# B units over 128 rows in a spectral layer and ELU kernel: Y regrouped from SBUF to SBUF

## The chip, the core and the metric

The kernel runs on one core of one Trainium2 chip. A time is the device microseconds of one execution. Before the change three runs took 894.23, 894.43 and 895.2 us; the median is 894.43 us.

## What is computed

Eight sequences of 3008 rows by 256 channels are transformed along the rows, mixed over channels by a complex matrix, shrunk, transformed back, and put through a two-layer network with an ELU between:

```python
X = np.fft.rfft(x, axis=1)
Yr = Xr @ w_r - Xi @ w_i + b_r
Yi = Xr @ w_i + Xi @ w_r + b_i
Y  = sign(Y) * max(|Y| - 0.01, 0)          # real and imaginary part each
y  = np.fft.irfft(Y, n=3008, axis=1)
h  = y @ w_in                              # 256 -> 2048
out = where(h > 0, h, exp(min(h, 0)) - 1) @ w_out   # 2048 -> 256
```

## The kernel before

3008 is 47 x 64, and each transform is done in two factors, as matrix products with small constant matrices M1 to M4. For one sequence (a "batch" here) the spectral part is a list of units, each a few matmuls and one move out of PSUM:

- A units (`unit_A`, L170 matmuls): first factor of the forward transform; stored to DRAM (DA) and loaded again as Z.
- X units (`unit_X`, L207): second factor; gives XT.
- M units (`unit_M`, q = 0..5, i = 0, 1; L247 in batch 1, L289 from batch 2 on): channel mixing and shrinking. The PSUM result goes through VectorE (L257, or L144 and L296) and then GpSimd (L269 and L270, or L301, L302 and L303), which writes one half of the tile Y(q): 128 partitions, two frequencies pp, real and imaginary part c, 256 channels.
- B units (`unit_B`, v = 0..5; L375): first factor of the inverse transform on Y(v). Partitions 0 to 63 of Y hold one parity s of the frequencies, 64 to 127 the other. The two parities are separate products over 64 rows; for each, the real and the imaginary part are added up in PSUM. That makes eight matmuls of 64 rows by 256 columns for a unit: 2 (pp) x 2 (c) x 2 (s). The result is copied to Bz (L144 or L146), every second unit stored to DRAM (DB, L400), and loaded again as Bs (`load_Bs`, L408) after unit B5.
- Y units (`unit_Y`, L538): second factor of the inverse transform; gives yT, the network's input.

The network runs in steps: one step is four matmuls of the first layer (`front`, L1006), exponential and ELU on ScalarE, VectorE and GpSimd (L1022 to L1061), and eight fp32 matmuls of the second layer (`back`, L1080), two steps later. There are 47 steps for a batch (`PER`), and every eighth one copies osb out of PSUM (L1092) and stores it (L1101).

The order is written out by hand in `plan(b)`: while the network works on batch b, the list `seq` gives to each step one unit of batch b + 1, or an A unit of batch b + 2. `f0[t]` holds what a step emits ahead of its first-layer matmuls, `f1[t]` what it emits between them and its second-layer matmuls. Every engine takes its instructions in the order in which they were emitted. All stores and most loads are issued by SyncE (SP); the loads of x (xt, L117) by GpSimd. SP's DMAs use eight completion semaphores in turn, and one of them may have to wait until the DMA eight places before it has landed.

PSUM for X, B, A and Y units is one buffer of two banks (`psF`, tag fps), so that a unit waits until the one before it has been copied out. Batch 0 is worked off ahead of the steps and has functions of its own (`split_B`, L426; `turn_B`, L470); they stay with 64 rows.

Of the kernel before, what the change touches and what calls it, by code (L numbers as in the profile page):

```python
# [20 lines left out]
N2 = 64  # L21
K1 = 24
# [7 lines left out]
def kernel(  # L30
# [25 lines left out]
    constp = ctx.enter_context(tc.tile_pool(name="constp", bufs=1))  # L56
    M1 = constp.tile([P, P], F32R, name="M1")
    M2 = constp.tile([2 * NR, NS, 2, 2 * K1], BF16, name="M2")
    M3 = constp.tile([P, K1 // 2, 2, P], BF16, name="M3")
# [6 lines left out]
    bias_p = constp.tile([P, 2 * D], BF16, name="bias_p")  # L66
# [10 lines left out]
    space = constp.tile([P, 384], BF16, name="space")  # L77
# [24 lines left out]
    Z_of = {}  # L102
    XT_of = {}
    Y_of = {}
    Bz_of = {}
    DB_of = {}
    Bs_of = {}
# [119 lines left out]

    def sum_of(dt, ch):

        return XS[:, 3 * dt + ch] if 3 * dt + ch < 5 else busy[:]  # L230

    def three_weights(c, dt):

# [6 lines left out]
    def m_group(b, q, i, ps, biased=False):  # L240
        XT = XT_of[b]
        o = (2 * q + i) * P
        todo = [(c, dt) for c in range(2) for dt in range(2)]
        if b == 0:
            todo.sort(key=lambda z: z[1])
        for c, dt in todo:
            nc.tensor.matmul(  # L247
                ps, lhsT=XT[:, dt, c, o : o + P], rhs=(wcat_r, wcat_s)[c][:, dt, :],
                start=(not biased and (c, dt) == (0, 0)), stop=((c, dt) == (1, 1)),
            )  # L250
        if i == 0:
            Y_of[b, q] = wk3.tile([P, 2, 2 * D], BF16, name="Y", tag="Y")
        if biased:
            yb = ps
        else:
            yb = wk3.tile([P, 2 * D], F32, name="yb", tag="yb")[:]
            nc.vector.tensor_tensor(yb, ps, bias_bc[:], ALU.add)  # L257
        if (b, q, i) == (0, 2, 0):
            clip = late3.tile([P, 2 * D], F32, name="gT", tag="gT")
        else:  # L260
            clip = wk2.tile([P, 2 * D], F32, name="clip", tag="clip")
        return yb, clip

    def unit_M(b, q, i):
        if b == 1:
            if i == 0:
                mps_of[q] = unit_ps("mps", False)
            yb, clip = m_group(b, q, i, mps_of[q][:, i, :])
            nc.gpsimd.tensor_scalar(clip[:], yb, LAM, -LAM, ALU.min, ALU.max)  # L269
            nc.gpsimd.tensor_tensor(Y_of[b, q][:, i, :], yb, clip[:], ALU.subtract)  # L270
            return
        XT, o = XT_of[b], (2 * q + i) * P
        if i == 0:
            Y_of[b, q] = wk3.tile([P, 2, 2 * D], BF16, name="Y", tag="Y")
# [12 lines left out]
        for out_, lhs, w in todo:  # L287
            for dt in range(2):
                nc.tensor.matmul(  # L289
                    out_, lhsT=lhs[:, dt] if lhs is not None else sum_of(dt, ch)[:, oc : oc + P],  # L290
                    rhs=w[:, dt, :], start=(dt == 0), stop=(dt == 1),
                )
# [10 lines left out]
        nc.gpsimd.tensor_tensor(Y_of[b, q][:, i, :], yb[:], clip[:], ALU.subtract)  # L303
# [30 lines left out]
    def last_M(q, i):  # L334
# [26 lines left out]
        for Y_, yb, ch in todo:  # L361
            nc.vector.scalar_tensor_tensor(Y_, yb, LAM, ch, ALU.add, ALU.min)

    def unit_B(b, v, alone=False, on_dve=False, all_dve=False):
        if (b, v // 2) not in Bz_of:
            t = "A" if alone and v == 0 else "Bz"
            Bz_of[b, v // 2] = wk2.tile([P, 8, D], BF16, name=t, tag=t)
            if b not in DB_of:
                DB_of[b] = dram.tile([K1, P, D], BF16, name="DB", tag="DB")
        Bz, Y = Bz_of[b, v // 2], Y_of.pop((b, v))  # L370
        ps = unit_ps("bps", alone)
        for pp in range(2):
            for c in range(2):
                for s in range(2):
                    nc.tensor.matmul(  # L375
                        ps[:, s, pp * D : pp * D + D],
                        lhsT=M3[s * N2 : s * N2 + N2, 2 * v + pp, c, :],
                        rhs=Y[s * N2 : s * N2 + N2, pp, c * D : c * D + D],
                        start=(c == 0), stop=(c == 1),
                    )  # L380
# [33 lines left out]
    def split_B(v, ps, on_dve=(False, True), by_half=False):  # L414
# [8 lines left out]
        def half(pp):  # L423
            for c in range(2):
                for s in range(2):
                    nc.tensor.matmul(  # L426
                        ps[s][:, pp * D : pp * D + D],
                        lhsT=M3[s * N2 : s * N2 + N2, 2 * v + pp, c, :],
                        rhs=Y[s * N2 : s * N2 + N2, pp, c * D : c * D + D],
                        start=(c == 0), stop=(c == 1),  # L430
                    )
# [22 lines left out]
    def turn_B(v, ts=(0, 1), ps=None, on_dve=False):  # L454
# [11 lines left out]
        for pp in range(2):  # L466
            for dt in ts:
                for c in range(2):
                    for s in range(2):
# [7 lines left out]
                            rhs=M3[s * N2 : s * N2 + N2, 2 * v + pp, c, :].rearrange(  # L477
                                "p (g m) -> p g m", g=4
                            )[:, :, 0:8],
                            start=(c == 0), stop=(c == 1),  # L480
# [69 lines left out]
    def idle_pe(n):  # L550

        for _ in range(n):
            nc.tensor.matmul(ips[:], lhsT=busy[:, 0:P], rhs=busy[:], start=True, stop=True)

    nc.vector.memset(bias_p[:], 0.0)
    bpd = dram.tile([3, 2 * D], BF16, name="bpd", tag="bpd")
    idle_pe(9)
# [272 lines left out]
    XS = sump.tile([P, 5, 512], BF16, name="XS")  # L830
# [60 lines left out]
    for o, src, sc, bi in ((1, w3, TURN, 0.0), (0, a3, -TURN, hpi[:])):  # L891
        if o == 0:
            nc.scalar.activation(a3[:], w3[:], AF.Abs)
        nc.scalar.activation(
            M3[:, :, 0, o * N2 : o * N2 + N2], src[:], AF.Sin, bias=bi, scale=sc
        )
    sgb = sg3[:].unsqueeze(2).to_broadcast([P, K1 // 2, N2])
    first_M(3, 0, True)
    nc.vector.scalar_tensor_tensor(
        M3[:, :, 1, 0:N2], M3[:, :, 0, N2:P], 2.0, sgb, ALU.mult, ALU.mult  # L900
    )
    nc.vector.scalar_tensor_tensor(
        M3[:, :, 1, N2:P], M3[:, :, 0, 0:N2], -2.0, sgb, ALU.mult, ALU.mult
    )
    first_M(3, 1, True)
    let_go()
# [203 lines left out]
    def plan(b):  # L1110
# [5 lines left out]
        mid = [("X", u) for u in range(8)] + [  # L1116
# [4 lines left out]
        ]  # L1121
        if n1 < B:
            if b:
                lead, xs = 0, (3, 6, 9) if b < 3 else (3, 8, 13)

                def M(q):
                    return [("M", q, 0), ("M", q, 1)]
# [1 line left out]
                shift = b - 1 if b < 3 else b - 3  # L1129
                seq = [("y", 2), ("y", 3)] + [None] * shift + [("X", u) for u in range(8)]  # L1130
                if b < 3:
                    seq += [("y", 4)] + M(0) + M(1) + [("y", 5), ("B", 0)]
                else:
                    seq += M(0) + [("y", 4)] + M(1) + [("y", 5), ("B", 0)]
                seq += M(2) + [("y", 6), ("B", 1)] + M(3) + [("y", 7), ("B", 2)]
                on_act = [("X", 4), ("X", 7), ("B", 3)] + [("y", u) for u in range(5, 8)]
                if b < 3:
                    on_act += [("A", 0)]
                    seq += M(4) + [("B", 3)] + M(5) + [("A", 0), ("B", 4), ("B", 5)]
                    seq += [("A", u) for u in range(1, 6)]  # L1140
                else:
                    on_act += [("y", 4), ("B", 4)]
                    seq += M(4) + [("B", 3), ("A", 0)] + M(5) + [("B", 4), ("A", 1), ("B", 5)]
                    seq += [("A", u) for u in range(2, 6)] + [None] * (3 if n2 == B else 2)
                seq += [("n", 0), ("n", 1)]
            else:
                lead, seq = FILL, (
                    [u for u in mid if u[0] != "A"]
                    + [("A", 0), ("A", 1), ("A", 2), ("n", 0), ("n", 1)]
                    + [("A", u) for u in range(3, 6)]  # L1150
                )
# [3 lines left out]
        for t, u in enumerate(seq, lead):  # L1155
# [16 lines left out]
                    f0[t].append(put("A", n2, u[1]))  # L1172
            else:
                f0[t].append(put(u[0], n1, *u[1:]))
            if u == ("B", 5):
                f1[t + (b > 0 and n2 < B)] += [
                    (load_Bs, (n1, w, 0, 4 * K1 - 16 * (b == w == 0))) for w in range(4)
# [4 lines left out]
        if b == 0:  # L1182
# [6 lines left out]
            f1[1].insert(0, (scale_w_in, (1, True, 1)))  # L1189
            for w in range(1, 4):  # L1190
                f1[w].append((load_Bs, (0, w)))
            f1[5] += [(load_Z, (1, s0, s1)) for s0, s1 in ((0, 8), (8, 16), (16, NS))]
            f1[xs[0]].append((lambda: gate(Z_of[1][:, 16, 0:1]), ()))
        if n2 < B:
# [94 lines left out]
```

## Time and profile before

| what | value |
| --- | --- |
| three runs | 894.23, 894.43, 895.2 us (median 894.43) |
| profiled execution: span from first to last instruction | 903.9 us (1.06% above the median; no other time is given for it) |
| mean granted TensorE clock | 0.948 |
| busy: TensorE, weight load, VectorE, ScalarE, GpSimd | 99%, 75%, 75%, 80%, 66% |
| matmuls of L375 (B units, 42 units) | 336, 25.9 us busy |
| stores and loads issued by SP (queue q1) | 76.64 MB, 30.0% of the engines' span |

All times in the text, unless said otherwise, are microseconds from the start of the span of this one profiled execution. "Busy" of TensorE adds up modelled ends of pipelined matmuls, so what a group costs is read from the start of its first matmul to the start of the next group's first.

### The profile page before, as it was taken

How to read it: one execution, taken by the hardware profiler on the slowest of the kernel's cores; microseconds unless marked ns; L12 is line 12 of the kernel's file. 1: busy time of each engine (PE TensorE's matmuls, PEld its weight loads, DVE VectorE, ACT ScalarE, POOL GpSimd, SP SyncE). 2: the span in 40 equal slices, each digit the busy share in tenths (PEclk: the TensorE clock that was granted, in tenths of full speed). 3: DMA queues.
4: the chain of work that ended last, by engine and by line, in shares of the span. 5: the costliest groups of instructions: out<-in, count | busy, mean ns of one | idle time of the engine just before them, and what ended most of it. 6: DMA issues, size and time to landing. Idle time of an engine off the chain costs nothing.

```text
span 903.9 us, 18292 instructions
## 1 busy us (share of the span) xinstructions
PE 891.3 (99%) x6917; PEld 675.2 (75%) x6917; DVE 679.6 (75%) x969; ACT 722.4 (80%) x1001; POOL 596.7 (66%) x806
## 2 busy tenths in 40 slices
PE   9999999999999999999999999999999999999997
PEld 3467667877788777877778777787777877777776
DVE  7788778688866887668866788677876678778776
ACT  6778778888978889798887988878887798776654
POOL 7562550788657886588756877559875697753664
PEclk9999999999999999999999999999999999999998
DMA  8996226631474115632265231643218201241111
GB/s 262 310 258 188 70 71 181 169 119 47 118 209 124 65 50 152 173 117 88 72 181 136 86 116 48 189 140 101 87 53 229 70 24 48 69 108 36 28 44 47
DMA packets 90718, 105.85 MB, mean 117 GB/s; under 512 B 5395, under 2 KB 81174, under 8 KB 87302
## 3 DMA queue, kind: packets, MB, share of 16 engines
q1 hardware_dynamic: 84278, 76.64, 30.0%
q0 software_dynamic: 5968, 27.26, 9.4%
q8 instruction: 54, 0.88, 0.4%
q10 hardware_dynamic: 384, 0.79, 0.3%
q14 instruction: 34, 0.28, 0.1%
HBM read 54.86 MB, written 49.81 MB: 116 GB/s over the span
## 4 chain that ended last, share of the span: by engine, by line
PE 90%; DVE 3%; DMA 3%; ACT 2%; POOL 1%; issue 1%; SPq 0%; DVEq 0%; ACTq 0%; POOLq 0%
PE ps_o L1080 37%; PE hps L1006 36%; PE mps L289 5%; PE bps L375 2%; PE xps L207 2%; PE yps L538 2%; PE aps L170 2%; DVE gT L1048 2%; PE mps L247 1%; DVE Bz L144 1%; DMA xt<-in_x_dram 1%; DMA Z<-DA 1%; DMA DB<-Bz 1%; PE sps L1006 1%; DMA DA<-A 0%
## 5 line engine op out<-in xcount | busy, mean ns | idle before, releaser
L1048 DVE SCALAR_TENSOR_TENSOR gT<-Et,hps 128x512 fp32r<-128x512 f32 (+1 forms) x544 | 423.7, 811 | 158.5 <-POOL Et L1059 115.4
L1080 PE MATMUL ps_o<-w_out_r,gT 128*128 128x256 f32 x3008 | 481.4, 303 | 0.0
L1080 PEld LDWEIGHTS ps_o<-w_out_r,gT 128*128 128x128 f32 x3008 | 407.7, 190 | 52.4 <-ACT osb L1092 0.5
L1059 POOL TENSOR_SCALAR Et<-Et 128x512 f32<-128x512 f32 x434 | 258.3, 614 | 223.6 <-ACT Et L1022 213.2
L1006 PE MATMUL hps<-yT,w_in_s 128*128 128x512 bf16 (+7 forms) x1688 | 388.9, 360 | 2.0 <-DVE gT L1048 1.3
L1022 ACT ACTIVATE Et<-hps 128x512 f32<-128x512 f32 x412 | 224.2, 598 | 67.8 <-PE hps L1006 63.3
L1006 PEld LDWEIGHTS <-w_in_s 128*128 128x128 bf16 x1728 | 144.7, 99 | 119.7 <-issue 21.7
L1024 ACT ACTIVATE Et<-hps 128x1024 f32<-128x1024 f32 x130 | 133.6, 1027 | 57.3 <-PE hps L1006 49.0
L1025 ACT ACTIVATE Et<-Et 128x1024 f32<-128x1024 f32 x130 | 137.4, 1057 | 4.1
L301 POOL TENSOR_TENSOR yb<-yb,bias_bc 128x512 f32<-128x512 f32 x72 | 92.3, 1282 | 9.5 <-DVE yb L296 9.4
L303 POOL TENSOR_TENSOR Y<-yb,clip 128x512 bf16<-128x512 f32 x72 | 92.6, 1286 | 6.0
L296 DVE TENSOR_TENSOR yb<-mps,yb 128x512 f32<-128x512 f32 x72 | 49.8, 692 | 7.6 <-PE hps L1006 0.5
L146 ACT CAST XT<-xps 128x768 bf16<-128x768 f32 x57 | 45.5, 799 | 9.8 <-PE xps L207 9.7
L146 ACT CAST A<-aps 128x1024 bf16<-128x1024 f32 x40 | 40.5, 1014 | 11.4 <-PE aps L170 9.9
L302 POOL TENSOR_SCALAR clip<-yb 128x512 f32<-128x512 f32 x72 | 44.2, 614 | 6.3
L289 PE MATMUL mps<-wcat_s,XT 128*128 128x256 bf16 x288 | 44.1, 277 | 0.0
L144 DVE COPY yb<-mps 128x256 f32<-128x256 f32 x72 | 30.3, 421 | 11.1 <-PE mps L289 9.7
L1050 DVE SCALAR_TENSOR_TENSOR gT<-hps,Et 128x1024 fp32r<-128x1024 f32 x29 | 35.5, 1223 | 2.4
L224 POOL TENSOR_TENSOR XS<-XT 128x512 bf16<-128x512 bf16 x30 | 34.1, 1159 | 2.1 <-ACT XT L146 1.2
L1092 DVE COPY osb<-ps_o 128x512 f32<-128x512 f32 x46 | 31.6, 686 | 1.2 <-PE ps_o L1080 0.5
L146 ACT CAST Bz<-bps 128x1024 bf16<-128x1024 f32 x32 | 31.9, 998 | 0.5 <-PE bps L375 0.4
L1027 ACT ACTIVATE Et<-hps 128x1024 f32<-128x1024 f32 x29 | 29.8, 1029 | 2.6 <-PE hps L1006 1.2
(184 smaller groups left out, 678.8 us busy)
## 6 DMA issues: line engine op xcount, KB each, us to landing
xt<-in_x_dram POOLq DMA_DIRECT2D x21, 1024.0 KB, 5.4
out_dram<-osb SPq DMA_DIRECT2D x158, 128.0 KB
Bs<-DB SPq DMA_DIRECT2D x30, 384.0 KB
DB<-Bz SPq DMA_DIRECT2D x20, 512.0 KB
DA<-A SPq DMA_DIRECT2D x19, 512.0 KB
Z<-DA SPq DMA_DIRECT2D x5, 1152.0 KB
Z<-DA SPq DMA_DIRECT2D x11, 384.0 KB
xt<-in_x_dram POOLq DMA_DIRECT2D x6, 512.0 KB, 6.0
```

Of the source, the lines that this page charges most:

```text
L146: nc.scalar.copy(dst, src)
L289: nc.tensor.matmul(out_, lhsT=lhs[:, dt] if lhs is not None else sum_of(dt, ch)[:, oc : oc + P], rhs=w[:, dt, :], start=(dt == 0), stop=(d ...
L296: nc.vector.tensor_tensor(yb[:].rearrange("p (c d) -> p c d", c=2), ps[:].rearrange("p (c d) -> p c d", c=2), yb[:, D : 2 * D].unsqueeze(1 ...
L301: nc.gpsimd.tensor_tensor(yb[:], yb[:], bias_bc[:], ALU.add)
L303: nc.gpsimd.tensor_tensor(Y_of[b, q][:, i, :], yb[:], clip[:], ALU.subtract)
L1006: nc.tensor.matmul(hps[s][:, c0:c1] if early else hps[:, s, c0:c1], lhsT=w_in_s[:, dt, ft * P : ft * P + P], rhs=yT_of[b][:, dt, t0 : t0 + ...
L1022: nc.scalar.activation(E_[:, s], hps[:, s], AF.Exp)
L1024: nc.scalar.activation(E_, hps[:], AF.Relu, scale=-1.0)
L1025: nc.scalar.activation(E_, E_, AF.Exp, scale=-1.0)
L1048: nc.vector.scalar_tensor_tensor(o, e, -1.0, h, ALU.add, ALU.max)
L1059: nc.gpsimd.tensor_scalar(E_[s], E_[s], 1.0, 0.0, ALU.min, ALU.max)
L1080: nc.tensor.matmul(po[q][:, i_ % 2, :], lhsT=gT[:, s, i_ * P : i_ * P + P], rhs=w_out_r[:, ft, :], start=(ft == 0 and i_ % 2 == 0), stop=( ...
```

## The change

`turn_Y(b, q)` takes a finished Y(q) and writes a second tile Yx with four SBUF to SBUF DMAs, issued by SP. In Yx the real part of a parity lies on partitions 0 to 63 and the imaginary part on 64 to 127, so that the sum over both is one product over 128 rows. A B unit then has four matmuls of 128 rows by 256 columns, with no adding up in PSUM. The constant M3 is split in two tiles and regrouped once in the same way into M3x (`turn_M3`, in step 6 of batch 0). `turn_Y` is emitted in `f1` of the step behind M(q, 1). Y and Yx share a ring of four buffers (Y had three).

In the order of the units, some B units go a step later. Batch 1: B3 to B5 all come behind M(5, 1). Batches 2 and 3: B0 comes behind M(2, 0), and B5 behind A1. Batches 4 to 7: B5 comes behind A2. Tiles move between pools so that the memory suffices: `bias_p` takes a buffer of the Bs ring, `XS` and one half of M3 share a buffer, the other half takes an osb buffer, and `space` shrinks.

```diff
+    def by_part(dst, of):
+        for c in range(2):
+            for s in range(2):
+                nc.sync.dma_start(dst[c * N2 : c * N2 + N2, :, s, :], of(c, s))
+
+    def turn_M3():
+        by_part(M3x, lambda c, s: M3[c][s * N2 : s * N2 + N2])
+
+    def turn_Y(b, q):
+        Y = Y_of.pop((b, q))
+        Yx_of[b, q] = Yx = wk4.tile([P, 2, 2, D], BF16, name="Yx", tag="Y")
+        by_part(Yx, lambda c, s: Y[s * N2 : s * N2 + N2, :, c * D : c * D + D])
...
         for pp in range(2):
-            for c in range(2):
-                for s in range(2):
-                    nc.tensor.matmul(
-                        ps[:, s, pp * D : pp * D + D],
-                        lhsT=M3[s * N2 : s * N2 + N2, 2 * v + pp, c, :],
-                        rhs=Y[s * N2 : s * N2 + N2, pp, c * D : c * D + D],
-                        start=(c == 0), stop=(c == 1),
-                    )
+            for s in range(2):
+                nc.tensor.matmul(
+                    ps[:, s, pp * D : pp * D + D], lhsT=M3x[:, 2 * v + pp, s, :],
+                    rhs=Yx[:, pp, s, :], start=True, stop=True,
+                )
...
-            ("M", 4, 1), ("B", 3), ("M", 5, 0), ("M", 5, 1), ("B", 4),
-            ("A", 0), ("B", 5), ("A", 1), ("A", 2), ("A", 3), ("A", 4),
+            ("M", 4, 1), ("M", 5, 0), ("M", 5, 1), ("B", 3), ("B", 4), ("B", 5),
...
                 if b < 3:
-                    seq += [("y", 4)] + M(0) + M(1) + [("y", 5), ("B", 0)]
+                    seq += [("y", 4)] + M(0) + M(1) + [("y", 5)]
+                    seq += [("M", 2, 0), ("B", 0), ("M", 2, 1)]
...
-                    seq += M(4) + [("B", 3)] + M(5) + [("A", 0), ("B", 4), ("B", 5)]
-                    seq += [("A", u) for u in range(1, 6)]
+                    seq += M(4) + [("B", 3)] + M(5) + [("A", 0), ("B", 4), ("A", 1), ("B", 5)]
+                    seq += [("A", u) for u in range(2, 6)]
...
-                    seq += M(4) + [("B", 3), ("A", 0)] + M(5) + [("B", 4), ("A", 1), ("B", 5)]
-                    seq += [("A", u) for u in range(2, 6)] + [None] * (3 if n2 == B else 2)
+                    seq += M(4) + [("B", 3), ("A", 0)] + M(5) + [("B", 4), ("A", 1), ("A", 2), ("B", 5)]
+                    seq += [("A", u) for u in range(3, 6)] + [None] * (3 if n2 == B else 2)
...
+            if u[0] == "M" and u[2] == 1:
+                f1[t + 1].append((turn_Y, (n1, u[1])))
...
+            f1[6].append((turn_M3, ()))
```

More of the change, by code (lines that the diff above doesn't have):

```diff
@@ L58 @@
     M2 = constp.tile([2 * NR, NS, 2, 2 * K1], BF16, name="M2")
-    M3 = constp.tile([P, K1 // 2, 2, P], BF16, name="M3")
+    M3x = constp.tile([P, K1 // 2, 2, P], BF16, name="M3x")
     M4 = constp.tile([4 * K1, 2 * N1], BF16, name="M4")
@@ L65 @@
     bias_bc = constp.tile([P, 2 * D], F32, name="bias_bc")
-    bias_p = constp.tile([P, 2 * D], BF16, name="bias_p")
     lam_n = constp.tile([P, 1], F32, name="lam_n")
@@ L76 @@
     idm = constp.tile([P, P], BF16, name="idm")
-    space = constp.tile([P, 384], BF16, name="space")
+    space = constp.tile([P, 128], BF16, name="space")
     dram = ctx.enter_context(tc.tile_pool(name="dram", bufs=2, space=bass.MemoryType.DRAM))
@@ L104 @@
     Y_of = {}
+    Yx_of = {}
+    M3 = []
+    XS_of = []
     Bz_of = {}
@@ L228, in sum_of @@
     def sum_of(dt, ch):
-        return XS[:, 3 * dt + ch] if 3 * dt + ch < 5 else busy[:]
+        if 3 * dt + ch == 5:
+            return busy[:]
+        if not XS_of:
+            XS_of.append(sump.tile([P, 5, 512], BF16, name="XS", tag="XS"))
+        return XS_of[0][:, 3 * dt + ch]
     def three_weights(c, dt):
@@ L251, in m_group @@
         if i == 0:
-            Y_of[b, q] = wk3.tile([P, 2, 2 * D], BF16, name="Y", tag="Y")
+            Y_of[b, q] = wk4.tile([P, 2, 2 * D], BF16, name="Y", tag="Y")
         if biased:
@@ L273, in unit_M @@
         if i == 0:
-            Y_of[b, q] = wk3.tile([P, 2, 2 * D], BF16, name="Y", tag="Y")
+            Y_of[b, q] = wk4.tile([P, 2, 2 * D], BF16, name="Y", tag="Y")
         ps, k1 = (
@@ L369, in unit_B @@
                 DB_of[b] = dram.tile([K1, P, D], BF16, name="DB", tag="DB")
-        Bz, Y = Bz_of[b, v // 2], Y_of.pop((b, v))
+        Bz, Yx = Bz_of[b, v // 2], Yx_of.pop((b, v))
         ps = unit_ps("bps", alone)
         for pp in range(2):
-            for c in range(2):
-                for s in range(2):
-                    nc.tensor.matmul(
-                        ps[:, s, pp * D : pp * D + D],
-                        lhsT=M3[s * N2 : s * N2 + N2, 2 * v + pp, c, :],
-                        rhs=Y[s * N2 : s * N2 + N2, pp, c * D : c * D + D],
-                        start=(c == 0), stop=(c == 1),
-                    )
+            for s in range(2):
[3 more added lines that the diff above has]
+                )
         o = 4 * (v % 2)
@@ L427, in half @@
                         ps[s][:, pp * D : pp * D + D],
-                        lhsT=M3[s * N2 : s * N2 + N2, 2 * v + pp, c, :],
+                        lhsT=M3[c][s * N2 : s * N2 + N2, 2 * v + pp, :],
                         rhs=Y[s * N2 : s * N2 + N2, pp, c * D : c * D + D],
@@ L476, in turn_B @@
                             ],
-                            rhs=M3[s * N2 : s * N2 + N2, 2 * v + pp, c, :].rearrange(
+                            rhs=M3[c][s * N2 : s * N2 + N2, 2 * v + pp, :].rearrange(
                                 "p (g m) -> p g m", g=4
@@ L553, in idle_pe @@
             nc.tensor.matmul(ips[:], lhsT=busy[:, 0:P], rhs=busy[:], start=True, stop=True)
+    bias_p = wk4.tile([P, 2 * D], BF16, name="bias_p", tag="Bs")
     nc.vector.memset(bias_p[:], 0.0)
@@ L829 @@
     sump = ctx.enter_context(tc.tile_pool(name="sump", bufs=1))
-    XS = sump.tile([P, 5, 512], BF16, name="XS")
+    M3.append(sump.tile([P, K1 // 2, P], BF16, name="M3", tag="XS"))
+    M3.append(late2.tile([P, K1 // 2, P], BF16, name="M3", tag="osb"))
     w_in_v = moe_w_in.rearrange("(c p) f -> p c f", p=P)
@@ L894 @@
         nc.scalar.activation(
-            M3[:, :, 0, o * N2 : o * N2 + N2], src[:], AF.Sin, bias=bi, scale=sc
+            M3[0][:, :, o * N2 : o * N2 + N2], src[:], AF.Sin, bias=bi, scale=sc
         )
@@ L899 @@
     nc.vector.scalar_tensor_tensor(
-        M3[:, :, 1, 0:N2], M3[:, :, 0, N2:P], 2.0, sgb, ALU.mult, ALU.mult
+        M3[1][:, :, 0:N2], M3[0][:, :, N2:P], 2.0, sgb, ALU.mult, ALU.mult
     )
     nc.vector.scalar_tensor_tensor(
-        M3[:, :, 1, N2:P], M3[:, :, 0, 0:N2], -2.0, sgb, ALU.mult, ALU.mult
+        M3[1][:, :, N2:P], M3[0][:, :, 0:N2], -2.0, sgb, ALU.mult, ALU.mult
     )
@@ L1131, in plan @@
                 if b < 3:
-                    seq += [("y", 4)] + M(0) + M(1) + [("y", 5), ("B", 0)]
-                else:
-                    seq += M(0) + [("y", 4)] + M(1) + [("y", 5), ("B", 0)]
-                seq += M(2) + [("y", 6), ("B", 1)] + M(3) + [("y", 7), ("B", 2)]
+                    seq += [("y", 4)] + M(0) + M(1) + [("y", 5)]
+                    seq += [("M", 2, 0), ("B", 0), ("M", 2, 1)]
+                else:
+                    seq += M(0) + [("y", 4)] + M(1) + [("y", 5), ("B", 0)] + M(2)
+                seq += [("y", 6), ("B", 1)] + M(3) + [("y", 7), ("B", 2)]
                 on_act = [("X", 4), ("X", 7), ("B", 3)] + [("y", u) for u in range(5, 8)]
@@ L1147, in plan @@
                 lead, seq = FILL, (
-                    [u for u in mid if u[0] != "A"]
+                    mid
                     + [("A", 0), ("A", 1), ("A", 2), ("n", 0), ("n", 1)]
```

## The prediction, on record before the changed kernel was run

> **What bounds the kernel now.** I read the page's busy shares first, then the chain that ended last, then TensorE's timeline around a B unit of batch 5.
>
> ```profile
> PE 891.3 (99%) x6917; PEld 675.2 (75%) x6917; DVE 679.6 (75%) x969; ACT 722.4 (80%) x1001; POOL 596.7 (66%) x806
> ...
> PE 90%; DVE 3%; DMA 3%; ACT 2%; POOL 1%; issue 1%; SPq 0%; DVEq 0%; ACTq 0%; POOLq 0%
> ```
>
> TensorE is never long idle and holds 90% of the chain. So time taken off its instruction stream comes off the end, and a wait put into that stream (it runs in order) is added to the end.
>
> ```profile
> 559.58 0.28 PE L289 MATMUL mps<-wcat_r,XS 128*128 128x256 bf16 x1
> 559.70 0.27 PE L289 MATMUL mps<-wcat_r,busy 128*128 128x256 bf16 x1
> 559.81 0.62 PE L289 MATMUL mps<-wcat_s,XT 128*128 128x256 bf16 x4
> 560.25 1.07 PE L1006 MATMUL hps<-yT,w_in_s 128*128 128x512 bf16 x4
> 560.96 1.30 PE L1080 MATMUL ps_o<-w_out_r,gT 128*128 128x256 f32 x8
> 562.20 0.62 PE L375 MATMUL bps<-Y,M 64*128 64x256 bf16 x8
> 562.75 1.07 PE L1006 MATMUL hps<-yT,w_in_s 128*128 128x512 bf16 x4
> 563.46 1.28 PE L1080 MATMUL ps_o<-w_out_r,gT 128*128 128x256 f32 x8
> 564.58 0.62 PE L170 MATMUL aps<-xt,M 128*128 128x512 f32 x2
> 565.26 1.05 PE L1006 MATMUL hps<-yT,w_in_s 128*128 128x512 bf16 x4
> 565.95 1.30 PE L1080 MATMUL ps_o<-w_out_r,gT 128*128 128x256 f32 x8
> 567.18 0.62 PE L375 MATMUL bps<-Y,M 64*128 64x256 bf16 x8
> 567.73 1.06 PE L1006 MATMUL hps<-yT,w_in_s 128*128 128x512 bf16 x4
> ```
>
> Read starts, not durations. Eight B matmuls take 562.20 to 562.75, 0.55 us. Six full-height matmuls of the same 256 columns (L289) take 559.58 to 560.25, 0.67 us, 0.112 each. The eight fp32 matmuls ahead of a B unit take 560.96 to 562.20, 1.24; ahead of an A unit 563.46 to 564.58, 1.12. Over the whole timeline the medians are: B unit 0.549 (42 times); L1080 ahead of B 1.230, ahead of M, X, Y and A units 1.135, 1.133, 1.130 and 1.123.
>
> **Part 1, the matmuls: -8.3 us.** Four full-height matmuls at 0.113 (0.677/6) take 0.451 instead of 0.549, which saves 0.098. The extra ahead of the unit (1.230 less 1.130 = 0.100) is seen ahead of no group with 96 or 128 rows, so I let it go as well. 42 units x 0.198 = 8.3 us. Bounds: 0 if both excesses stay with the unit, 4.1 if only one goes. I take the full sum, because M, X, Y and A units around it are all without the excess. What is late next in a B step? It becomes 0.451 + 0.703 + 1.130 = 2.28 us; an A step (0.464 + 0.703 + 1.123 = 2.29) already carries the same ScalarE load (a copy of 1.01 and the exponential), and TensorE does not wait in it. So nothing takes the gain back there.
>
> Eight matmuls in 0.55 means that the two 64-row halves already run beside each other (one after the other they would need 8 x 0.113 = 0.90). [...]
>
> **Part 2, the new wait: +4 us.** A B unit now waits for: Y's last GpSimd instruction, four DMA issues on SP, the landing. I compared the end of each Y(q, 1) write (GpSimd's timeline, L270 and L303) with the start of its B unit:
>
> ```profile
> 564.42 1.29 POOL L303 TENSOR_TENSOR Y<-yb,clip 128x512 bf16<-128x512 f32 x1
> ```
>
> That is Y5 of batch 5, done at 565.71; B5 starts at 567.18: slack 1.47. All slacks before, B0 to B5: batch 1: 4.5, 6.9, 6.9, 6.9, 6.9, 1.6; batches 2 and 3: 3.7, 7.0, 7.9, 6.4, 6.6, 1.5; batches 4 to 7: 5.5, 8.3, 8.6, 6.2, 6.7, 1.5. The new order adds a step to B0 of batches 2 and 3 (6.2) and to every B5.
>
> *Price of a turn.* No SBUF to SBUF DMA is in this trace. SP issues a store of 128 partitions in 0.36 to 0.41 us (DB, DA), the ragged out stores in 0.54 to 0.85; plus 0.05 between two. Landings, from issue to the last update of the DMA's semaphore: out stores of 16 x 8 KB 2.3, a Bs load of 16 rows 2.0, a DB store of 256 KB 2.5, of 512 KB 3.2. A turn's DMA has 64 KB in 512-byte runs, so the smallest rows are nearest. Wake 0.06 + 3 x 0.5 + 2.1 = 3.7 us. Cheapest 0.06 + 3 x 0.42 + 1.8 (an estimate: 2.0 less the DRAM side) = 3.1; dearest 0.06 + 3 x 0.9 + 3.2 = 6.0.
>
> *B5, batches 2 to 7.* The inserted A step brings 2.29, the B units between give back 0.3 (their savings pull B5 forward): slack 1.5 + 2.0 = 3.5. In batch 7 the A steps are empty (703 + 1130 ns): about 3.1. Stall 0.2 x 5 + 0.6 = 1.6 us.
>
> *B5, batch 1.* Now M(5,1), B3, B4, B5. SP meets B3's store first, which waits for B3's copy: ScalarE finishes the M step's two passes 1.3 us after a B unit's start (L1025, 134.17 + 1.06 against 133.94), the copy takes 1.0. Store issued 2.35 after B3's start, the turn from 2.8 on, landed at about 6.2 to 6.4. B5 could start 4.8 after B3 (two steps and the buffer wait seen at 136.66). Stall 1.4.
>
> *B0, batches 5 and 6.* GpSimd issues an xt load just when Y0 is done:
>
> ```profile
> 518.09 1.28 POOL L303 TENSOR_TENSOR Y<-yb,clip 128x512 bf16<-128x512 f32 x1
> 519.32 0.58 POOL L117 DMA_DIRECT2D xt<-in_x_dram  x1
> ...
> xt<-in_x_dram POOLq DMA_DIRECT2D x1, 1024.0 KB, 6.4
> ```
>
> An out store that SP issued at 519.67 landed at 526.06 instead of after 2.3: its queue moved no packet from 521.5 to 523.5, while xt's queue ran. The turn is issued at 519.4 to 521.4, so I let it land at 525.8; B0 was at 525.18. Stall 0.6 x 2 = 1.2. [...]
>
> All other turns have slack of 4.4 or more against 3.7. Sum of stalls: 1.6 + 1.4 + 1.2 = 4.2.
>
> **Part 3, costs that I set at nothing.** SP: 168 issues of about 0.5 us spread over 47-step batches; out stores queued behind a turn's wait are late by at most some 4 us, and osb has two buffers for stores 16 steps (36 us) apart. The turn's 11 MB in 42 x 4 DMAs lie in the slices where the page shows DMA at 1 to 3 tenths. `turn_M3`: 3072 runs of 256 bytes, by the DB store's 1024 runs in 3.2 us an estimated 10 us from about 70 us on, behind the Z loads; first needed at 102. B5 a step later: in batches 2 and 3 Bs had landed 4.3 and 3.5 us ahead of its first Y unit (253.5, 362.9); one step less leaves 2.0 and 1.2, which hides it, but barely; if Bs lands 2 us later than now, this costs up to 1 us twice. Batches 4 to 7 keep 2 us or more.
>
> **Sum.** -8.3 + 4.2 = -4.1 us on a span of 903.9. The runs' median is 894.43, 1.06% shorter; a sum this small isn't changed by that. 894.4 - 4.1 = **890.3 us**.
>
> **Rivals.**
> - *All turns in time* (turn 3.1 us, xt collision absorbed): stalls of 0 to 1, 886.1 to 887. For it: the slack of 3.5 is just above the cheap price. Against: batch 1's queue on SP and the 6.4 us landing.
> - *The turn is dear.* Place: B5 of each batch, in TensorE's own order. It decides from about 4.5 us a turn: at 5.0 the B5 stalls are 1.5 x 5 + 1.9 + 2.7, B0 of batches 1, 5 and 6 wait 0.6, 1.2 and 1.2, together 15; less 8.3 this gives 901 us, slower. For it: no row shows this kind of DMA, and the ragged stores cost 0.85 to issue. At the dear end, 6.0, it is about 912. Against: four rows of 2.0 to 2.5 us for small transfers.
> - *The matmuls don't get as short as that*: only one excess goes, -4.1 + 4.2: 894.5, no change. Against: all neighbours of full height are without it.
>
> **How the numbers follow.** Forecast (887.5 to 892.6) 0.60; all in time 0.17; no change 0.11; dear 0.12. Within 0.2% means within 1.8 us, about what a measurement can tell from no change. Faster 0.77, same 0.11, slower 0.12. The range, 886.0 to 896.0, takes in the first three and the start of the fourth; what lies above is left out with about 0.1, and a rest on both ends.
>
> **What would show it.** Right: four matmuls of a B unit 0.45 from start to start, L1080 ahead of them 1.13 where nothing waits; TensorE waits for the Yx DMAs at B5 of batch 1 (over 1 us) and by tenths at the others; B0 of batches 5 and 6 waits for a landing near xt's. Wrong: waits of over 1 us at every B5, a turn's landing above 3 us, the 1.23 ahead of B still there with the data in place, or a wait for Bs at 253 and 363.

## The result and the profile after

The changed kernel takes **906.1 us** (median of four runs, 904.12 to 906.59); the kernel before, on the same chip, 894.33. The ratio is 1.0127, 95% interval 1.0113 to 1.0142: slower by 11.8 us, where 4.1 us faster was forecast, and above the range of 886.0 to 896.0.

One thing about the profile that the prediction was read from: its execution ran at a granted clock of 0.948 throughout (span 903.9), while the timed runs of the same kernel run at 0.999 or so. The kernel before was therefore profiled again (run e0 below: span 892.7, clock 1.000, time 894.62); all comparisons here are with that execution. The profiled run of the changed kernel took 904.12, span 902.3, clock 0.997. Lines in the text are of the changed kernel: the first layer L1006 is now L1025, the second L1080 is L1099, B's matmuls are L394, GpSimd's Y write is L309, its clamp of the exponential L1078, the turn's DMAs L374, the out stores L1120.

Busy shares and the chain that ended last, of the changed kernel:

```profile
PE 876.3 (97%) x6749; PEld 674.1 (75%) x6749; DVE 681.3 (76%) x969; ACT 722.5 (80%) x1001; POOL 596.3 (66%) x806
...
PE 69%; POOL 11%; DMA 5%; DVE 5%; ACT 3%; issue 3%; SPq 2%; DVEq 0%; POOLq 0%; ACTq 0%
```

TensorE held 89% of the chain in e0 and holds 69% now. GpSimd, DMAs and SP's queue (SPq) have come in. What TensorE waits for (us in total, times, longest):

```profile
PE bps L394 <- DMA Yx<-Y: 8.7, 12, 2.0
PE hps L1025 <- DVE gT L1067: 6.7, 15, 1.8
```

In e0 there is no first row, and the second one (there L1006 and L1048) is 2.0 us in 6 waits. This table counts from the modelled end of a matmul. Counted from start to start, against 1.13 us for the second layer ahead of a B unit and 0.447 for the unit, what the B units wait for Yx comes to about 11 us.

TensorE's timeline at B2 of batch 5, where the data is in place, and at B5, which has to wait:

```profile
542.74 1.02 PE L1025 MATMUL hps<-yT,w_in_s 128*128 128x512 bf16 x4
543.41 1.27 PE L1099 MATMUL ps_o<-w_out_r,gT 128*128 128x256 f32 x8
544.52 0.61 PE L394 MATMUL bps<-Yx,M3x 128*128 128x256 bf16 x4
544.97 1.03 PE L1025 MATMUL hps<-yT,w_in_s 128*128 128x512 bf16 x4
...
567.58 1.27 PE L1099 MATMUL ps_o<-w_out_r,gT 128*128 128x256 f32 x8
568.70 0.28 PE L394 MATMUL bps<-Yx,M3x 128*128 128x256 bf16 x1
569.30 0.50 PE L394 MATMUL bps<-Yx,M3x 128*128 128x256 bf16 x3 [0.32 <-DMA Yx<-Y]
569.63 1.03 PE L1025 MATMUL hps<-yT,w_in_s 128*128 128x512 bf16 x4
```

B2: 544.52 to 544.97, 0.45 us, and the second layer ahead of it 543.41 to 544.52, 1.11. Both excesses are gone. B5: one matmul can go, then the unit waits for the last landing and lasts 0.93.

### The profile page after: what moved, and what is told of

Same layout as the page of the kernel before. It is cut to its first block, busy times and chain, and to the rows that moved or that the text cites. A ratio compares the mean times of both kernels' runs of the same rounds, so it can differ in the third digit from the quotient of the medians.

```text
span 902.3 us, 18251 instructions
## 1 busy us (share of the span) xinstructions
PE 876.3 (97%) x6749; PEld 674.1 (75%) x6749; DVE 681.3 (76%) x969; ACT 722.5 (80%) x1001; POOL 596.3 (66%) x806
## 4 chain that ended last, share of the span: by engine, by line
PE 69%; POOL 11%; DMA 5%; DVE 5%; ACT 3%; issue 3%; SPq 2%; DVEq 0%; POOLq 0%; ACTq 0%
PE ps_o L1099 29%; PE hps L1025 28%; POOL Y L309 4%; POOL yb L307 3%; DMA Yx<-Y 3%; PE mps L295 3%; PE xps L209 2%; SPq L374 2%; PE yps L555 2%; POOL clip L308 2%; PE bps L394 1%; DVE gT L1067 1%; PE aps L172 1%; PE mps L253 1%; DVE osb L1111 1%
## 5 line engine op out<-in xcount | busy, mean ns | idle before, releaser
L1099 PE MATMUL ps_o<-w_out_r,gT 128*128 128x256 f32 x3008 | 477.4, 302 | 0.0
L1099 PEld LDWEIGHTS ps_o<-w_out_r,gT 128*128 128x128 f32 x3008 | 404.5, 189 | 48.9 <-DVE osb L1111 1.2
L1078 POOL TENSOR_SCALAR Et<-Et 128x512 f32<-128x512 f32 x434 | 258.4, 614 | 228.4 <-ACT Et L1041 218.4
L1025 PE MATMUL hps<-yT,w_in_s 128*128 128x512 bf16 (+7 forms) x1688 | 378.0, 352 | 7.2 <-DVE gT L1067 6.7
L1025 PEld LDWEIGHTS <-w_in_s 128*128 128x128 bf16 x1728 | 146.2, 98 | 116.5 <-issue 18.9
L1043 ACT ACTIVATE Et<-hps 128x1024 f32<-128x1024 f32 x130 | 133.5, 1027 | 53.0 <-PE hps L1025 47.1
L309 POOL TENSOR_TENSOR Y<-yb,clip 128x512 bf16<-128x512 f32 x72 | 92.6, 1286 | 6.0
L394 PE MATMUL bps<-Yx,M3x 128*128 128x256 bf16 x168 | 27.3, 275 | 8.9 <-DMA Yx<-Y 8.7
```

Of the source, the lines that this page charges most:

```text
L1025: nc.tensor.matmul(hps[s][:, c0:c1] if early else hps[:, s, c0:c1], lhsT=w_in_s[:, dt, ft * P : ft * P + P], rhs=yT_of[b][:, dt, t0 : t0 + ...
L1043: nc.scalar.activation(E_, hps[:], AF.Relu, scale=-1.0)
L1078: nc.gpsimd.tensor_scalar(E_[s], E_[s], 1.0, 0.0, ALU.min, ALU.max)
L1099: nc.tensor.matmul(po[q][:, i_ % 2, :], lhsT=gT[:, s, i_ * P : i_ * P + P], rhs=w_out_r[:, ft, :], start=(ft == 0 and i_ % 2 == 0), stop=( ...
```

## The experiments

The kernel before ran beside each group on the same chip: 894.86 us with e0 to e3, 894.5 with e4 to e7, 893.8 with e8 and e9, 893.96 with e10 and e11. Ratios are to those.

**e0, the kernel before again** (no edit).

> The kernel before, unchanged, profiled once more. The profile on which the prediction was built had a granted clock of 0.948 and a span of 903.9 us, though the timed runs took 894.4. If the clock explains the difference: a span of about 892.5 us at a clock near 0.997, with a B unit still at 0.55 us and the fp32 matmuls ahead of it 0.1 us longer than ahead of other units. Rival (the 0.1 us on both sides belonged to the lower clock): the excess is gone at full clock, and then the 128-row form has little to gain.

894.62 us, span 892.7, clock 1.000. B unit 0.543 from start to start, second layer ahead of it 1.219, ahead of other units 1.11 to 1.13: the two excesses that the prediction counted are there at full clock too (0.096 and 0.086 against the 0.447 and 1.133 of the changed kernel).

**e1, the matmuls alone**: the kernel before, with B's eight matmuls replaced by

```diff
+            for s in range(2):
+                nc.tensor.matmul(
+                    ps[:, s, pp * D : pp * D + D], lhsT=M3[:, 2 * v + pp, s, :],
+                    rhs=Y[:, pp, s * D : s * D + D], start=True, stop=True,
+                )
```

> Order, buffers and Y of the kernel before; only the B units of batches 1 to 7 have four matmuls of 128 rows instead of eight of 64, straight from Y. It leaves out the regrouping, so that the products are not those of the reference. Theory (the matmul term of the prediction was right, the losses lie in waits): 42 x 0.19 = 8 us less than before, 886 us, ratio 0.991. Rival (the saving is not on the path or not there): within 2 us of before.

890.49 us, 0.9957 (0.9944 to 0.9971): 4.4 us faster, a little over half of the 8 expected. In the profiles, from the first X unit of the steps to the end, TensorE needs 811.8 us instead of 815.9 in e0, 4.1 less; at the B units themselves, start to start, it is 6.7 us shorter. Part of that comes back as waits of the first layer for gT, in the table of TensorE's waits of e1:

```profile
PE hps L1003 <- DVE gT L1045: 3.5, 14, 0.6
```

against 2.0 in 6 waits in e0: 1.5 of the missing 2.6 us. The rest shows where an M unit follows a B unit. ScalarE's and TensorE's timelines of e1 at B2 of batch 5, which starts at 537.86:

```profile
539.15 0.99 ACT L146 CAST Bz<-bps 128x1024 bf16<-128x1024 f32 x1
```

```profile
538.98 1.30 PE L1077 MATMUL ps_o<-w_out_r,gT 128*128 128x256 f32 x8
540.19 0.27 PE L289 MATMUL mps<-wcat_r,XS 128*128 128x256 bf16 x1
```

ScalarE's copy of the B unit ends at 540.14 and the M unit starts 0.05 us later. M's PSUM buffers take the same banks (`last_banks` opens one pool in the place of the other), so M has to wait for that copy. There are 22 M units behind a B unit that ScalarE copies: in e1 all of them start 0.050 to 0.052 us after the end of the copy, in e0 0.14 to 0.19. The second layer ahead of these 22 is 1.4 us longer in sum. (The two counts are taken in different ways and overlap by some tenths.)

**e2, the order alone**: the kernel before with only the new lists of units.

```diff
-                    seq += [("y", 4)] + M(0) + M(1) + [("y", 5), ("B", 0)]
+                    seq += [("y", 4)] + M(0) + M(1) + [("y", 5)]
+                    seq += [("M", 2, 0), ("B", 0), ("M", 2, 1)]
```

(and the same moves of B3 to B5 as in the change).

> The kernel before with nothing but the new order of the units (B0 of batches 2 and 3 behind M(2,0), B5 a step later, B3 to B5 of batch 1 behind M(5,1)); 64-row matmuls straight from Y, no DMA. Theory (in batches 2 and 3 the B0 step has its ELU on GpSimd and now stands behind M(2,0) and a sum of XT there, so that TensorE waits about 2.2 us for it in each): 4 to 5 us slower than before, 899 us. Rival (the order costs nothing, as the prediction had it, and all of the loss is the wait for Yx): within 1 us of before.

896.8 us, 1.0024 (1.0014 to 1.0034): 1.9 us slower, with nothing regrouped; 4 to 5 were expected. TensorE's timeline of e2 names the place, the step of Y6, two steps behind B0 of batch 2 (and the same in batch 3):

```profile
206.20 1.02 PE L1006 MATMUL hps<-yT,w_in_s 128*128 128x512 bf16 x3 [1.56 <-DVE gT L1048]
```

GpSimd's timeline of the changed kernel at the same place tells why:

```profile
202.41 1.16 POOL L226 TENSOR_TENSOR busy<-XT 128x512 bf16<-128x512 bf16 x1
203.53 1.28 POOL L307 TENSOR_TENSOR yb<-yb,bias_bc 128x512 f32<-128x512 f32 x1
204.89 0.61 POOL L308 TENSOR_SCALAR clip<-yb 128x512 f32<-128x512 f32 x1
205.59 1.30 POOL L309 TENSOR_TENSOR Y<-yb,clip 128x512 bf16<-128x512 f32 x1
206.84 1.19 POOL L1078 TENSOR_SCALAR Et<-Et 128x512 f32<-128x512 f32 x2
```

A B0 step lets GpSimd clamp the exponential (L1078). With M(2,0) now ahead of B0, a partial sum and M's three operations stand in front of that clamp. VectorE's gT waits for the clamp (1.66 us there), the next first layer waits until gT has read its PSUM buffer (1.74), and TensorE stands from 207.1 to 208.8 in the changed kernel. From start to start the two waits are 1.7 and 1.8 us in e2. That the whole kernel loses only 1.9 is because smaller waits elsewhere are gone, such as 0.3 us ahead of B5 of batch 1 and of B1 of batches 2 and 3 in e0.

**e3, the turn unread**: the changed kernel with all its DMAs and its order, but B reads Y.

```diff
-                    rhs=Yx[:, pp, s, :], start=True, stop=True,
+                    rhs=Y[:, pp, s * D : s * D + D], start=True, stop=True,
```

> The changed kernel with all its DMAs and its order, but the B units read Y, not Yx (four matmuls of 128 rows; the products are not those of the reference). So the DMAs run and nobody on TensorE waits for them. Theory (waits for Yx cost about 11 us, the order 4 to 5, the traffic nothing): -8 + 4.5 = 891 us, 15 us below the changed kernel less some that the waits hide. Rival (the DMAs' traffic and SP's time are the loss): stays near 900 to 906.

897.03 us, 1.0017 (1.0007 to 1.0027), between the 891 of the theory and the 900 to 906 of the rival. From e1 (-4.4) and e2 (+1.9) 892.4 would follow, if the two add up. The 4.7 us above that come with the transfers (and with the moved tiles), though no B unit waits for Yx. TensorE's timeline shows one wait behind it, Y0 of batch 2 for Bs, because SP had the turn of B5, the DB stores and four out stores in one row ahead of its loads (e2, the same order without the turns, has no such wait):

```profile
144.07 0.79 PE L555 MATMUL yps<-M,Bs 96*128 96x94 bf16 x8 [2.51 <-DMA Bs<-DB]
```

and something that I had not reckoned with, TensorE's clock right behind this wait. These are stretches of 2 us (behind the length, TensorE's busy time; third from the end, the granted clock):

```profile
142.00:144.00 2.00, 0.00 (x0) 0.00 (x0) 1.70 (x2) 0.00 (x0) 0.00 (x0) 0.92 0.91 242
144.00:146.00 2.00, 1.70 (x11) 1.12 (x13) 0.00 (x0) 0.79 (x1) 0.00 (x0) 0.50 1.02 219
146.00:148.00 2.00, 2.00 (x19) 1.86 (x18) 0.34 (x1) 1.03 (x1) 0.00 (x0) 0.73 1.02 280
```

For 3.41 us (143.66 to 147.08) half the clock is granted. The other such stretch of this execution, 208.52 to 211.93, follows the wait for gT at Y6 of batch 2, so I put it down to the order and not to the transfers. Two such stretches are worth an estimated 3.4 us (half of 2 x 3.41). From the first X unit of the steps on, TensorE needs 819.1 us here, 5.5 more than e0's with the differences of e1 and e2; the wait for Bs and the two stretches come to 5.9. e3's eleven runs lie apart accordingly: 894.2 to 896.0 us at a mean clock of 0.999 to 1.000 (four runs, median 894.6, 2.2 above 892.4), 896.1 to 898.1 at 0.996 to 0.998 (seven). So about half of the 4.7 is clock.

**e4, slack**: the changed kernel with three edits of its plan.

```diff
-                lead, xs = 0, (3, 6, 9) if b < 3 else (3, 8, 13)
+                lead, xs = 0, (3, 6, 9) if b < 3 else (3, 8, 20)
...
-                    seq += [("y", 4)] + M(0) + M(1) + [("y", 5)]
-                    seq += [("M", 2, 0), ("B", 0), ("M", 2, 1)]
+                    seq += [("y", 4)] + M(0) + M(1) + [("y", 5), ("y", 6), ("B", 0)] + M(2)
...
-                    seq += M(4) + [("B", 3), ("A", 0)] + M(5) + [("B", 4), ("A", 1), ("A", 2), ("B", 5)]
+                    seq += M(4) + [("B", 3), ("A", 0)] + M(5) + [("B", 4), ("A", 1), ("A", 2), ("A", 3), ("B", 5)]
```

(and B5 of batches 2 and 3 in the same way; an empty step more ahead of Y0 keeps its distance to B5)

> The changed kernel with three edits of its plan. B0 of batches 2 and 3: the step of Y6 goes ahead of B0 in place of M(2,0). The third xt load of batches 4 to 7 goes from step 13 to step 20. Every B5 of batches 2 to 7 moves one A step further back. Theory (TensorE pays each wait in place, so a wait that is taken away is gained): in the changed kernel's profile these places cost 2 x 2.2 us (the ELU behind GpSimd's queue at B0 of batches 2 and 3), 3.7 (B0 of batches 5 and 6 behind the xt load) and 4.1 (B5 of batches 2 to 7), together 12; 906 less 12 gives 894, and 892 to 896 with the start of the kernel as it falls. Rival 1 (most of the loss is traffic and SP load, which the order does not change): above 900. Rival 2 (the waits come back at the next unit): 897 to 902, with new waits in the same batches.

897.3 us, 1.0028 (1.0018 to 1.0037): 8.8 us of the 12 are gained, so most of the theory holds and rival 1 falls. What TensorE still waits for, from the table of its waits in e4:

```profile
PE bps L394 <- DMA Yx<-Y: 3.7, 5, 2.0
PE hps L1025 <- DVE gT L1067: 3.3, 12, 0.6
PE yps L555 <- DMA Bs<-DB: 1.7, 2, 1.2
```

The last row is new, as rival 2 would have it for a part: with B5 two steps later than before, Bs is late in batches 2 and 3 (0.67 and 1.33 us from start to start). The longest is B5 of batch 1, whose order e4 leaves as it was.

**e5, B0's order alone, and e6, the xt load alone**: the second and the first of these edits by themselves.

> Only the first of the three edits: in batches 2 and 3, Y6 ahead of B0 in place of M(2,0), so that GpSimd has nothing queued ahead of the exponential's clamp of B0's step, while Y0's transfers keep their extra step. Theory: the two waits of 1.9 and the two of 0.3 behind them go, 4.4 us, 901.5. Rival (the step after takes it back): less than 1.5 us.

902.88 us, 1.0094 (1.0080 to 1.0109): 3.2 us less than the changed kernel. The waits of 1.9 us are gone, 0.4 and 0.7 are left in their place.

> Only the second edit: the third xt load of batches 4 to 7 at step 20 in place of step 13, so that it is not in flight with the transfers of Y0 of batches 5 and 6. Theory: those land 4.1 us after Y's end, B0 waits for nothing, 3.7 us less, 902.4. Rival (the transfers are slow there for another reason, such as an out store): B0 still waits, no change.

902.67 us, 1.0081 (1.0061 to 1.0101): 3.4 us less, and B0 of batches 5 and 6 waits for nothing. So xt's load was what delayed the turn there. In the changed kernel GpSimd issues it at 518.92, right behind the write of Y, and TensorE's timeline at B0 shows

```profile
525.43 0.70 PE L394 MATMUL bps<-Yx,M3x 128*128 128x256 bf16 x4 [0.89 <-DMA Yx<-Y]
```

The trace's semaphore updates, which tell when a transfer has landed, put the four landings at 6.0 to 6.6 us (batch 5) and 6.1 to 8.1 us (batch 6) after Y's end, against 2.1, 2.7, 3.4 and 4.0 in the 21 turns of the changed kernel that nothing disturbs.

**e7, two transfers for four**:

```diff
+        for c in range(2):
+            nc.sync.dma_start(Yx[:, :, c, :], Y[:, :, c * D : c * D + D])
```

> The changed kernel with each turn of Y as two transfers of 128 partitions and 128 KB in place of four of 64 partitions and 64 KB (the same bytes; the rows are not regrouped, so B's products are not the reference's). Theory (the turn's length is issues in series, 0.65 each, plus one landing of 2.1): it ends at about 2.8 us after Y's end instead of 4.1, the B5 waits of batches 2 to 7 (4.1 in all) go, that of batch 1 is shorter by 1.3, and SP has 84 issues fewer: 6 us less, 900. Rival (the landing grows with the bytes and each transfer waits for the one before): it ends at 3.8 or more, within 1.5 us of the changed kernel.

898.03 us, 1.0035 (1.0022 to 1.0047): 8 us less than the changed kernel, more than the 6 expected. By the semaphore updates a turn with SP free ends 2.8 to 3.0 us after Y's end, with twice the bytes in each transfer; B5 of batches 2 to 7 no longer waits, but for 0.1 us in batch 4. In these two kernels a turn's length is issues in series and one landing (0.03 + 3 x 0.65 + 2.05 us with four transfers), and the landing is nearly the same for 64 KB (2.05 us) and 128 KB (2.2).

**e8, e4 with one more empty step ahead of Y0 in batches 2 and 3**.

> The slack kernel (three edits of the plan) with one more empty step ahead of Y0 of the next batch in batches 2 and 3, because its profile shows Y waiting there for Bs (0.67 and 1.33 us). Theory (each wait is paid in place): 2 us less than the slack kernel's 897.3, 895.3; what is left above the matmuls-alone kernel is batch 1 (B5 2.65) and the SP load. Rival (the Bs wait was only where another wait showed): no change, 897.

897.27 us, 1.0034 (1.0022 to 1.0047): no gain. The wait for Bs is gone, but the first layer now waits about 1.0 us in each of the two batches for yT, the product of the Y units that came later. The rival was right.

**e9, e8 with half of each turn (and of M3x's) issued by GpSimd**:

```diff
-                nc.sync.dma_start(dst[c * N2 : c * N2 + N2, :, s, :], of(c, s))
+                (nc.gpsimd if c else nc.sync).dma_start(dst[c * N2 : c * N2 + N2, :, s, :], of(c, s))
```

> The same plan, with two of the four transfers of a turn issued by GpSimd (which has just written Y) and two by SP. Theory (issues in series set the turn's length): last landing about 2.8 us after Y's end in place of 4.1 (one issue of 0.65 and one landing of 2.1), also where SP is busy with stores for half of the transfers; B5 of batch 1 waits about 1 us less, B0 of batch 1 and B5 of batch 7 nothing; 893 to 894. Rival (GpSimd pays: two issues of 0.6 us or more a turn lie ahead of the clamp of the next step's exponential, as M's chain did in batches 2 and 3): new waits for gT, 897 or more.

913.03 us, 1.0219 (1.0202 to 1.0236). The turn did end at 3.1 us, but the rival decided. GpSimd's timeline, then TensorE's:

```profile
213.65 1.29 POOL L309 TENSOR_TENSOR Y<-yb,clip 128x512 bf16<-128x512 f32 x1
215.23 1.24 POOL L374 DMA_DIRECT2D Yx<-Y  x2 [0.29 <-POOL Y L309]
216.50 1.19 POOL L1078 TENSOR_SCALAR Et<-Et 128x512 f32<-128x512 f32 x2
```

```profile
218.49 0.59 PE L1025 MATMUL hps<-yT,w_in_s 128*128 128x512 bf16 x1 [2.52 <-DVE gT L1067]
```

Two issues of 0.62 us each and a wait of 0.29 stand ahead of the clamp, and TensorE's waits for gT rise to 14.6 us, from 3.3 in e8. The runs' clock of 0.993 to 0.997 takes part of the rest.

**e10, e4 with work in the wait**: eight matmuls of no use ahead of B5 of batch 1, into its own PSUM tile.

```diff
+        if (b, v) == (1, 5):
+            for _ in range(8):
+                nc.tensor.matmul(
+                    ps[:, 0, :], lhsT=w_in_s[:, 0, 0:P], rhs=w_in_s[:, 0, 0 : 2 * D],
+                    start=True, stop=True,
+                )
```

> The slack kernel with eight matmuls of no use (0.21 us each, written to B5's own PSUM tile and overwritten by it) ahead of B5 of batch 1, where TensorE waits 2.2 us for its transfers. The slack kernel's twelve runs lie apart by their granted clock: 895.3 to 896.6 at 0.998 to 1.000, 898.0 to 899.2 at 0.997 to 0.998; in the changed kernel's trace the clock is 0.5 for 3.41 us from 2.6 us after this wait ended or so (136.4 to 139.8). Theory (a wait of about 2 us in TensorE makes the gate grant half the clock for one window of 3.41 us, 1.7 us lost, in some runs and not in others): with work in the wait, all runs are at 0.999 or so and the median is 895.5, though TensorE has more to do. Rival (the clock has another cause): the runs split as before, median 897 to 898.

894.82 us, 1.0008 (0.9999 to 1.0017): against the kernel before, 0.0020 or 1.8 us less than e4, with more to do. Ten of the twelve runs are at a clock of 0.999 or more (e4: five), two at 0.997 and 0.998. The profiled execution is one of the two: its half clock lies at 47.8 to 51.3 us, behind a wait of 2.8 us ahead of the steps, which the fill does not touch; at B5 of batch 1 its clock is full. So the theory holds for the place that was filled, on the evidence of the runs' clocks. Two figures of the expectation are off: the wait in e4 is 2.6 us from start to start, and the half clock in the changed kernel begins at 136.4, 1.4 us after B5's first matmul. The filled wait in TensorE's timeline of e10 (one of the eight is missing from the records):

```profile
137.11 1.89 PE L394 MATMUL bps<-w_in_s 128*128 128x512 bf16 x7
139.14 0.28 PE L400 MATMUL bps<-Yx,M3x 128*128 128x256 bf16 x1
139.78 0.50 PE L400 MATMUL bps<-Yx,M3x 128*128 128x256 bf16 x3 [0.35 <-DMA Yx<-Y]
140.11 1.03 PE L1031 MATMUL hps<-yT,w_in_s 128*128 128x512 bf16 x4
```

**e11, e10 with two more edits of the plan**: the last partial sum of XT in the step of Y6, and B5 of batch 7 an empty step later.

> The same with two more edits of the plan: in batches 2 and 3 GpSimd's sum of the last chunk of XT goes from the step of M(2,0) to the step of Y6, where GpSimd has nothing else (M's wait for gT of 0.65 us, twice); in batch 7 B5 goes one empty A step further back (1.04 us wait for its transfers). Theory: 2.3 us less than the kernel without these two, 893 to 893.5, just under the kernel before. Rival (other waits take their place): 895 or more.

**893.0 us**, 0.9991 (0.9982 to 0.9999), 893.96 for the kernel before beside it. This is the best version with the regrouping, and 1 us faster than the kernel before, about half of the 0.2% that the prediction called measurable.

## Why the prediction was wrong

From the runs, the 11.8 us come together as: matmuls -4.4 (e1), order +1.9 (e2), transfers while no B unit waits for them +4.7 (e3 less these), waits for Yx +9.6 (the changed kernel less e3), each from medians beside the kernel before and good to about 1 us. The forecast had -8.3, 0, 0 and +4.2. So four steps failed: that nothing takes the matmuls' gain back, that order and traffic cost nothing, and the size of the waits. Every term missed to the same side. The last two differences would share otherwise if taken in another order, because B5's wait in the changed kernel covers the wait for Bs.

- **Part 1, the matmuls.** The mechanism was right: both excesses go, 0.096 and 0.086, together 0.18 for a unit and 7.6 us for 42 instead of 8.3. Four matmuls of 128 rows take 0.447 and eight of 64 rows 0.543: 1.65 times as many in the same time, where at 2 times the unit itself would have gained nothing. (In the first profile of the kernel before, the eight start in pairs, 3 to 4 ns apart within a pair and 0.11 us from pair to pair.) The step that failed is "nothing takes the gain back there": of 6.7 us gained at the units in e1, 4.1 arrived. The prediction took an A step as its measure, where ScalarE's copy mostly ends 1.7 us after the unit's start. Behind the exponential's two passes B's copy ends 2.2 us after it in e0 and 2.3 in e1, and the M unit behind waits for it.
- **Part 2, the price of a turn.** 3.7 us forecast; 4.0 to 4.1 where nothing disturbs it. The issue was mis-sized: 0.60 and 0.05 between two, so 0.65 three times over ahead of the last landing, where 0.5 was taken; the landing, 2.05 us, was right. (The cheapest price took 1.8, less than a Bs load's 2.0; the runs show no such gain.) The rival of a dear turn (decides from 4.5) does not hold for an undisturbed turn; that 906 lies between its 901 and 912 is no support for it.
- **B5, batches 4 to 6**: 0.51, 0.47, 0.43 us against 0.2; batch 7 1.33 against 0.6; batches 2 and 3 1.09 and 0.26 against 0.2. In batches 4 to 6 the 0.3 to 0.4 us of the turn carry over nearly one to one; in batch 2 the last landing came 0.7 us late, in batch 7 0.5 because one issue took 1.1 us.
- **B5, batch 1**: 2.64 against 1.4. The queue ahead of it on SP was right: the turn was issued at 131.04, 2.8 us after B3's start. The last landing came 7.3 us after B3's start instead of 6.2 to 6.4: one issue took 1.0 us, so that the four needed 2.35 to the last one's start instead of 1.5, and the landings were 2.1 to 3.1 us instead of 2.1.
- **B0, batches 5 and 6**: 1.15 and 2.65 against 0.6 each. The place and the cause were right (e6). In batch 5 the last landing came 6.6 us after Y's end (forecast 6.4), in batch 6 8.1, and B0 was ready earlier than taken. What the DMA queues moved in batch 5, in 520.0 to 522.5 (first line) and in 522.5 to 523.5, by number of packets, MB and share (q0 has xt's load, q1 what SP issues):

```profile
q0 software_dynamic: 75, 0.61, 91.2%
q0 software_dynamic: 43, 0.35, 90.6%
q1 hardware_dynamic: 37, 0.02, 9.5%
```

  The turn was issued from 519.01 on and moved nothing until 522.5, then nearly one packet of 512 bytes for one of xt's 8 KB. Why it moved nothing up to then stays open.
- **Other turns**, set at no wait: B0 of batch 1 waits 0.29 us, because its turn landed 4.5 us after Y's end.
- **Part 3, the order at nothing.** This failed outright (+1.9, e2). I had looked at what a moved B unit waits for, and not at what its step then leaves to GpSimd behind M's operations.
- **Part 3, SP and traffic at nothing.** Bs in batches 2 and 3 was hidden, as said: no wait there in the changed kernel; with one more step (e4) it was no longer. Bs of batch 1, which the prediction did not look at, is late in e3. In the changed kernel B5's own wait covers it. By e3's profile and runs its +4.7 are this wait and the clock, about half each.
- **The clock** was in no step. Stretches of 2 us of the changed kernel around B5 of batch 1 (columns as in e3):

```profile
132.00:134.00 2.00, 0.90 (x8) 0.70 (x6) 1.61 (x3) 1.70 (x2) 0.00 (x0) 1.00 0.85 245
134.00:136.00 2.00, 0.77 (x5) 0.50 (x6) 1.65 (x2) 0.00 (x0) 0.00 (x0) 1.00 0.52 132
136.00:138.00 2.00, 2.00 (x9) 1.50 (x8) 0.00 (x0) 1.74 (x2) 0.00 (x0) 0.59 0.77 209
138.00:140.00 2.00, 2.00 (x9) 1.34 (x9) 1.56 (x2) 0.47 (x2) 0.00 (x0) 0.56 0.80 249
140.00:142.00 2.00, 2.00 (x15) 1.47 (x14) 0.54 (x2) 1.79 (x2) 0.00 (x0) 1.00 0.70 191
```

  The trace has the clock at 0.5 from 136.4 to 139.8: a wait of 2.64 us is paid with an estimated 1.7 us on top (half of 3.41). From B5's first layer to the next one it takes 3.76 us, where 2.27 is usual. All four runs of the changed kernel have a mean clock of 0.996 or 0.997; profiled executions with one such stretch are at 0.997 or 0.998, with two at 0.996.

What stays open: why xt's load holds up SP's transfers for over 2 us, and why some issues on SP take 1.0 us instead of 0.6.

## What to carry to other kernels

When TensorE is the bound and its waits are near zero, a shorter unit saves only what the other engines can follow (4.1 of 6.7 us in e1), and a new dependency costs its tail at every place where the slack is within a few tenths of its price: price it from issue times in series plus one landing (here 0.65 us for each issue and 2.05), and check the queue in front of the issuer at each place, not once. Moving a unit by a step moves the work of its step on every engine (1.9 us in e2); look at what is queued ahead of the operation on which the next buffer depends. Where a buffer passes from one unit to the next, the copy out of it bounds the shorter unit too (0.05 us from its end to the next unit, 22 times in e1). Look at the clock behind a wait of TensorE: behind the 2.64 us at B5 of batch 1 of the changed kernel it was 0.5 for 3.41 us, an estimated 1.7 us more (half of 3.41); with the wait filled, in e10, it was full there.

## What the runs showed of the hardware

- **What stood ahead of a half clock.** In the changed kernel the clock is at 0.5 for 3.41 us, from 136.35 to 139.76. With time cut into stretches of that length counted back from the drops, and the ends of the kernels left out, the half clock followed stretches in which TensorE was idle by 0.52, 0.53, 0.54 (three times), 0.59, 0.61, 0.65, 0.67 and 0.80, and did not follow 0.45 (twice), 0.49, 0.50 and, twice in the changed kernel, 0.53. The same wait came with a half clock and without: B5 of batch 1 waits 2.64 us both in the changed kernel (0.67 of a stretch, half clock behind it, an estimated 1.7 us, half of 3.41) and in e4 (0.45, full clock). What decides between the two was not shown; that it is the idle share of such a stretch is the author's estimate from these numbers.
- **SBUF to SBUF transfers**: 0.60 us of issue on SP, 0.65 from issue to issue, 2.05 us to the landing of 64 KB, 2.2 of 128 KB, with nothing else under way; in the changed kernel the four of a turn landed 6.0 to 8.1 us after Y's end in the two turns (B0 of batches 5 and 6) that were issued together with GpSimd's load of 1 MB. Of the 33 others that SP issued right behind Y's end, the last landing came after 4.0 to 4.1 us in 21 and after 4.2 to 5.6 us in 12, with single issues of up to 1.3 us or landings of up to 4.0 among them.
- **One execution at 0.948 throughout**, the first profile of the kernel before: its span is 903.9 us against 892.7 at 1.000, 1.3% for 5% of clock.
